# A one-token attention and MLP kernel on one core: wq loaded ahead of the first K group, masked blocks summed on VectorE, and eight more unused matrix products

## The chip, the core and the metric

The kernel runs on one core of one Trainium2 chip. The metric is the device time of one execution in microseconds; the time before is the median of three runs, 193.28 us (193.27 to 193.34). A profiled execution of the same kernel took 193.18 us; its trace spans 191.9 us from the first to the last instruction, so 1.28 us of the time lies outside the span.

## What is computed

Eight requests, one new token each, go through an attention block with a sliding window over cached K and V, and then through a token-mixing MLP. Cut to what matters (LN is a layer norm without weights):

```
q = LN(x) @ wq                                 # 8 x 512 by 512 x 4096: 32 heads of 128
k, v = k_cache[:, :, -2048:], v_cache[...]     # 8 requests x 8 kv heads x 2048 x 128, bf16
p = softmax(q . k / sqrt(128));  o = p . v     # 4 query heads share a kv head
h = x + o @ wo
# B block with one token: the shifted parts are zero, so hs = 0 and x1 = LN(h)
h2 = x1 + gelu(LN(x1) @ w3) @ w4               # 512 x 1792 and 1792 x 512
out = h + h2
```

The core reads 79.18 MB from HBM, nearly all of it K and V, and writes 8 KB.

## The kernel before

**Loads.** SyncE's queue (SP) issues every large load, one after another in program order, with a wait only where a buffer must first come free. K and V come in 16 groups each (four kv heads of one request, 2.10 MB); K has three buffers (`knat`), V has three (`vnat`). The order is the string at L777: the first K group, then wq (one large transfer into `wbig`, and six small ones into `wqF` that carry the last 1152 columns), then two more K groups, then V and K in turn, then wo in three pieces, w3, and w4 in three pieces (eight, four and two blocks of 128 rows). `load_k` (L745) waits until the TensorE transposes of the group three before are done, `load_v` (L750) until the P V products of the group three before are done, `load_wo` (L755) for the q products, `load_w3` (L767) for the transposes of q.

**K.** A group is four items. For each item TensorE transposes the K tile (`pe_T`, L374, eight products at L383), ScalarE evicts the lower half (L393) and VectorE the upper half (L395), and TensorE multiplies with q (`pe_QK`, L398). Every engine runs its instructions in the order of the source. The first four items' transposes (`AHEAD`, L606 to L608) stand in this order ahead of `q_rows` and `q_turn`, which compute q, scale it and transpose it (L278 to L344); `fill` (L346) puts q into its block form on GpSimd.

**Softmax and P V.** After eight items a request's scores go through `softmax_1` to `softmax_4` on VectorE and ScalarE, `turn_P` and `widen` bring P into place, and `pe_PV` (L497) makes 16 products with a V group. The result bank holds four blocks of 128 columns, of which a row needs one. VectorE multiplies with a mask (L514), two GpSimd additions sum the four blocks (L516, L517), and the sum `oacc` goes to `pe_O` (L526). For the last request VectorE does it in four instructions instead (L519, L522).

**The end.** After the last P V come the wo products (L553, L574), the mean and the squares over the features (L652, L683: products with ones), the 56 products with w3 (`pe_w3`, L673), the activation (L702 on VectorE, L704 on ScalarE), and the 56 products with w4 (L731) in three calls, one for each piece of w4, with eight products between the first and the second call that add the rest of the result (`pe_fin`, L717). Four copies (L741, L743) and one small store end the kernel.

**Unused products.** `warm` (L482) and `warm_end` (L490) put 128 x 128 by 512 bf16 products into TensorE's order that nobody reads (L485, L493). They write a PSUM bank that is free there, and wait for no late event. Ahead of w3 there are two of them behind the squares (L685).

Of the kernel before, what the change touches and what calls it, by code (L numbers as in the profile page):

```python
# [8 lines left out]
ALU = mybir.AluOpType  # L9
AX = mybir.AxisListType  # L10
# [69 lines left out]
def bass_sequential_preLN__sliding_block_cached__mixer_s_mlp__decode_kernel(  # L80
# [23 lines left out]
    with es:  # L104
# [173 lines left out]
        def q_rows():  # L278
            for k, rows, n, at, where in fills():
                a = xln_b[:, :]  # L280
                cols = bass.AP(tensor=a.tensor, offset=a.offset + KC * at + KC - 1, ap=[a.ap[0], [KC, k], [KC * k, 4]])
                e_xP = DV.op(lambda e, cols=cols, where=where: e.tensor_copy(
                    xlnP[:, where].rearrange("b (e a) -> b e a", a=4), cols))

            def pe_fT(e):
                for k, rows, n, at, where in fills():
                    ins = e.matmul(fT_ps[rows, n * B:(n + 1) * B], xlnP[:, where], ident_b[0:B, 0:B],
                                   is_transpose=True, tile_position=(0, rows.start))
                return ins
            e = PE.op(pe_fT, e_xP)  # L290
            for k, rows, n, at, where in fills():
                e_fT = DV.op(lambda e, rows=rows, n=n: e.tensor_copy(xlnF[rows, n, 0:B], fT_ps[rows, n * B:(n + 1) * B]),
                             e, e_fz)
            out = []
            for j in range(2):
                def pe_q(e, j=j):
                    for kc in range(KC):
                        for u in range(4):
                            n = (4 * j + u) * R * DH
                            size = R * DH if kc < KC - 1 else max(0, min(R * DH, H * DH - QF - n))  # L300
                            if size:
                                ins = e.matmul(S_ps[j][32 * u:32 * (u + 1), 0:size], xlnT[:, kc, :], wq_v[:, kc, n:n + size],  # L302
                                               start=(kc == 0), stop=(kc == KC - 1 and size == R * DH),
                                               tile_position=(0, 32 * u), skip_group_check=True)
                    return ins

                def pe_qF(e):
                    for n in range(NF):
                        for u in range(4):
                            w = (u - 4) * R * DH + QF  # L310
                            lo = max(0, -w)
                            if lo < R * DH:
                                ins = e.matmul(S_ps[1][32 * u:32 * (u + 1), lo:R * DH], xlnF[:, n, :],
                                               wqF[:, n, w + lo:w + R * DH], start=False, stop=(n == NF - 1),
                                               tile_position=(0, 32 * u), skip_group_check=True)
                    return ins
                e_q = PE.op(pe_q, e_xT, (sem_wq, 16))
                if j == 1:
                    e_q = PE.op(pe_qF, e_fT, (sem_wf, 16 * len(FILL)))
                got = S_ps[j][:, :].rearrange("p (r d) -> p r d", r=R)  # L320
                for c in range(2):
                    if j == 0:
                        e = AC.op(lambda e, c=c, got=got: e.activation(qrow2[:, 0, :, c, :], got, ACT.Copy, scale=inv_sqrt_dh),
                                  e_q)
                    else:
                        e = DV.op(lambda e, c=c, got=got: e.tensor_scalar(qrow2[:, 1, :, c, :], got, inv_sqrt_dh, None,
                                                                          ALU.mult), e_q)
                out.append(e)
            return out, e_q
# [160 lines left out]
        def warm_end(count):  # L490
            def f(e):
                for n in range(count):
                    ins = e.matmul(kbank[1], ident_b[:, :], still, start=True, stop=True)  # L493
                return ins
            PE.op(f, e_pT[LAST, 1])

        def pe_PV(m):  # L497
            b, q = divmod(m, NQ)
            at, bank = bank_of(q)

            def f(e):
                for n in range(NN):
                    u = n % 2
                    ins = e.matmul(bank[64 * u:64 * (u + 1), :],  # L504
                                   pT_sb[:, b % 2, n, :].rearrange("p (x q) -> p q x", q=NQ)[:, q, :],
                                   v_tile(m)[:, n * 512:(n + 1) * 512], start=(n < 2), stop=(n >= NN - 2),
                                   tile_position=(0, 64 * u), skip_group_check=True)
                return ins
            e_PV[m] = PE.op(f, V(m), *(e_pT[b, x] for x in range(KQ)), free[at])
            acc = oacc[:, b % 2, q, :]  # L510
            if b < LAST:
                a = own_s[:, :]
                own = bass.AP(tensor=a.tensor, offset=a.offset, ap=[a.ap[0], [1, NS], [0, DH]])
                free[at] = DV.op(lambda e: e.tensor_tensor(omask[:, :, :], bank.rearrange("p (s d) -> p s d", s=NS), own,  # L514
                                                           ALU.mult), e_PV[m], e_acc.get(m - 1), e_own_s)
                e = PO.op(lambda e: e.tensor_tensor(omask[:, 0:2, :], omask[:, 0:2, :], omask[:, 2:4, :], ALU.add), free[at], pool[-1])  # L516
                pool[-1] = e_acc[m] = PO.op(lambda e: e.tensor_tensor(acc, omask[:, 0, :], omask[:, 1, :], ALU.add), e, e_O.get(b - 2))  # L517
                return
            e = DV.op(lambda e: e.tensor_scalar(acc, bank[:, 0:DH], own_s[:, 0:1], None, ALU.mult),  # L519
                      e_PV[m], e_O.get(b - 2), e_own_s)  # L520
            for s in range(1, NS):
                e = DV.op(lambda e, s=s: e.scalar_tensor_tensor(acc, bank[:, s * DH:(s + 1) * DH], own_s[:, s:s + 1], acc,  # L522
                                                                ALU.mult, ALU.add), e)
            e_acc[m] = free[at] = e
# [74 lines left out]
        def quad(f, q):  # L599
# [3 lines left out]
                   (5, each(widen, 2)), (5, each(warm, 1)), (5, each(widen, 3)), (6, each(warm, 2)), (6, each(warm, 1))),  # L603
                  ((6, quad(pe_PV, 0)), (7, quad(pe_PV, 1)), (11, late_O), (8, last_O)))
        LAG = (0, 0, 0, 0, 0, 0, KQ, -1)
        for p in range(AHEAD):  # L606
            pe_T(p)
            evict(p)  # L608
        e_qrow, e_q = q_rows()
        e_qT, e_qturn = q_turn()  # L610
        fill(0)
        fill(1)
        for p in range(NITEM + 24):
# [59 lines left out]
        def pe_w3(lo, hi, *waits):  # L673
            def f(e):
                for fc in range(lo, hi):
                    n, f = divmod(fc, FH)
                    for kc in range(KC):
                        ins = e.matmul(y_ps[n][:, f * B:(f + 1) * B],  # L678
                                       w3_cols(kc, fc),
                                       uT[:, kc * B:(kc + 1) * B], start=(kc == 0), stop=(kc == KC - 1))  # L680
                return ins
            return PE.op(f, *waits)
        e_st2 = PE.op(lambda e: e.matmul(st2, ones_f[:, :], hsq[:, :], start=True, stop=True), e_sq,  # L683
                      free[2])
        warm_end(2)  # L685
        e_y = [pe_w3(0, FH, e_u, (sem_w3, 16)), pe_w3(FH, FC)]

        e_vs = DV.op(lambda e: e.tensor_reduce(vsum[:, :], vr(st2), AX.X, ALU.add), e_st2)

# [36 lines left out]
        for n, waits in enumerate(((*e_gT, free[1]), (), ())):  # L726
            lo, hi = W4_AT[n:n + 2]
            def pe_w4(e, lo=lo, hi=hi):
                for fc in range(lo, hi):
                    for nb in range(KC):  # L730
                        ins = e.matmul(z_ps[32 * nb:32 * (nb + 1), :], gT[:, fc, :],  # L731
                                       w4_sb[:, fc, nb * 128:(nb + 1) * 128], start=(fc == 0), stop=(fc == FC - 1),
                                       tile_position=(0, 32 * nb), skip_group_check=True)
                return ins
            if n == 1:
                pe_fin()
            e_z = PE.op(pe_w4, (sem_w4[n], 16), *waits)
        for nb in range(KC):
            to, got = out_sb[:, nb * 128:(nb + 1) * 128], z_ps[32 * nb:32 * nb + B, :]
# [34 lines left out]
                B_w4[lo * 128:hi * 128, :].rearrange("(g p k) n -> p g (k n)", p=128, k=k), sem_w4[n])  # L774

        turn = {"K": 0, "V": 0, "O": 0}
        for kind in "KQKK" + 9 * "VK" + "VKKVKVKVVVOVOO":  # L777
            if kind == "Q":
                load_wq()
                continue  # L780
            {"K": load_k, "V": load_v, "O": load_wo}[kind](turn[kind])
            turn[kind] += 1
# [42 lines left out]
```

## Time and profile before

| | |
|---|---|
| median of three runs | 193.28 us (193.27 to 193.34) |
| profiled execution, its time | 193.18 us |
| its span | 191.9 us |
| busy: TensorE, VectorE, ScalarE, GpSimd | 151.5, 102.5, 95.7, 30.3 us |
| chain that ended last: transfers | 65% of the span |
| mean granted TensorE clock | 0.939 |
| GpSimd's two additions per P V (L516, L517) | 726 and 455 ns, 14 times each |
| VectorE's mask (L514) | 686 to 692 ns, 14 times |
| last wait for w3, and end of the 56 products with it | 185.07, 187.06 us |
| last products with w4 begin, end | 189.36, 189.77 us |
| store issued | 190.50 us |

How to read it: busy time of an engine is the time its instructions took, whatever they stood behind. The chain that ended last is followed back from the last instruction, at each step to what released it. Times in tables of stretches are microseconds from the start of the span. The granted clock is the share of full speed that TensorE's clock had.

### The profile page before, as it was taken

What the parts mean: (1) busy time and instruction counts of PE and PEld (TensorE: products, weight loads), DVE (VectorE), ACT (ScalarE), POOL (GpSimd) and SP (SyncE); (2) the same over time, 40 slices, a digit from 0 to 9 for tenths busy, and PEclk for the clock granted to TensorE, in tenths of its full rate; (3) what the DMA queues carried; (4) which work ended last, traced back from release to release, by engine and by line L of the source; (5) the groups of instructions that cost most, each with busy time, mean ns of one, the idle gap of its engine ahead of it and who ended that gap; (6) DMA issues with size and microseconds to landing.
All of it is one profiled execution on the core that took longest, in us unless ns stands there. A gap on an engine that the chain in (4) does not pass through costs nothing.

```text
span 191.9 us, 3209 instructions
## 1 busy us (share of the span) xinstructions
PE 151.5 (79%) x1325; PEld 94.9 (49%) x1325; DVE 102.5 (53%) x245; ACT 95.7 (50%) x124; POOL 30.3 (16%) x65
## 2 busy tenths in 40 slices
PE   0293879988878998699978896989898994777874
PEld 0281247664546555465655463746554661323453
DVE  2754314773386438543775275646853885535323
ACT  3081127776272927284559263754782767420331
POOL 8300020100230023002300230024002200140030
PEclk9999769999996999889999997999999999999985
DMA  6999999999999999999999999999999999999991
GB/s 220 422 406 432 437 420 427 434 437 424 434 429 427 430 430 427 429 430 430 437 430 420 437 430 429 420 437 424 437 434 425 434 434 432 408 430 428 411 409 75
DMA packets 6478, 79.38 MB, mean 414 GB/s; under 512 B 688, under 2 KB 704, under 8 KB 1856
## 3 DMA queue, kind: packets, MB, share of 16 engines
q1 hardware_dynamic: 6448, 79.18, 97.2%
q8 instruction: 10, 0.16, 0.3%
q14 instruction: 4, 0.03, 0.0%
q10 hardware_dynamic: 16, 0.01, 0.0%
HBM read 79.18 MB, written 0.01 MB: 413 GB/s over the span
## 4 chain that ended last, share of the span: by engine, by line
DMA 65%; PE 22%; DVE 6%; ACT 4%; SPq 1%; issue 1%; POOL 0%
DMA knat<-in_A_k_cache_dram 31%; DMA w_sb<-in_B_w_dram 16%; DMA vnat<-in_A_v_cache_dram 10%; PE kT_ps L383 9%; DMA wbig<-in_A_wq_dram 8%; PE S_ps L504 3%; ACT pT_sb L472 2%; PE S_ps L408 2%; PE o_rows L504 2%; DVE kT_sb L395 2%; ACT kT_sb L393 1%; PE S_ps L302 1%; PE sm L529 1%; PE kT_ps L678 1%; SPq L207 1%
## 5 line engine op out<-in xcount | busy, mean ns | idle before, releaser
L393 ACT ACTIVATE kT_sb<-kT_ps 128x1024 bf16<-128x1024 bf16 x64 | 65.6, 1025 | 65.3 <-PE kT_ps L383 65.2
L383 PE MATMUL kT_ps<-turn_f,knat 128*128 128x128 f32 x512 | 76.5, 293 | 12.2 <-DMA knat<-in_A_k_cache_dram 9.6
L383 PEld LDWEIGHTS kT_ps<-turn_f,knat 128*128 128x128 f32 x512 | 60.4, 149 | 31.9 <-issue 13.4
L395 DVE COPY kT_sb<-kT_ps 128x1024 bf16<-128x1024 bf16 x64 | 43.9, 686 | 34.7 <-PE kT_ps L383 34.6
L516 POOL TENSOR_TENSOR omask<-omask 128x256 f32<-128x256 f32 x14 | 10.2, 726 | 113.3 <-DVE omask L514 113.3
L408 PE MATMUL S_ps<-kT_sb,qblk 128*32 128x512 bf16 x256 | 26.5, 408 | 1.7 <-POOL qblk L350 1.1
L504 PE MATMUL o_rows<-vnat,pT_sb 128*64 128x512 bf16 x128 | 15.4, 381 | 5.4 <-ACT pT_sb L472 5.4
L472 ACT ACTIVATE pT_sb<-o_rows,own_f 128x512 bf16<-128x512 f32 x28 | 17.7, 694 | 1.8 <-PE o_rows L467 1.6
L504 PE MATMUL S_ps<-vnat,pT_sb 128*64 128x512 bf16 x112 | 13.4, 382 | 0.7 <-DMA vnat<-in_A_v_cache_dram 0.7
L504 PEld LDWEIGHTS o_rows<-vnat,pT_sb 128*64 128x64 bf16 x128 | 8.0, 109 | 11.5 <-issue 7.7
L408 PEld LDWEIGHTS S_ps<-kT_sb,qblk 128*32 128x32 bf16 x256 | 6.6, 93 | 13.4 <-issue 8.3
L514 DVE TENSOR_TENSOR omask<-o_rows,own_s 128x512 f32<-128x512 f32 x7 | 4.8, 686 | 12.5 <-PE o_rows L504 12.5
L514 DVE TENSOR_TENSOR omask<-S_ps,own_s 128x512 f32<-128x512 f32 x7 | 4.8, 692 | 11.7 <-PE S_ps L504 11.7
L350 POOL COPY qblk<-qT 64x64 bf16<-64x64 bf16 x16 | 5.0, 312 | 27.0 <-DVE qT L342 16.4
L504 PEld LDWEIGHTS S_ps<-vnat,pT_sb 128*64 128x64 bf16 x112 | 5.8, 110 | 6.8 <-issue 1.6
L529 PE MATMUL sm<-oacc,sel_o 128*128 128x256 f32 x16 | 7.2, 537 | 0.6 <-DVE oX L536 0.6
L440 ACT ACTIVATE E_sb<-S_ps,negM 128x512 f32<-128x512 f32 x8 | 5.5, 689 | 2.4 <-DVE negM L436 2.4
L259 PE MATMUL sm<-ident_b,xln_b 8*128 8x8 bf16 x4 | 0.3, 176 | 8.0 <-DVE xln_b L234 8.0
L517 POOL TENSOR_TENSOR oacc<-omask 128x128 f32<-128x128 f32 x14 | 6.4, 455 | 1.1
L559 ACT ACTIVATE orow<-kT_ps 128x512 bf16<-128x512 f32 x1 | 0.6, 597 | 11.2 <-PE kT_ps L553 11.2
L431 DVE TENSOR_REDUCE mblk<-S_ps 128x1 f32<-128x512 f32 x8 | 5.5, 682 | 0.8 <-PE S_ps L408 0.8
L453 DVE STREAM_TRANSPOSE PT_sb<-P_sb 128x512 bf16<-128x512 bf16 x8 | 5.6, 702 | 0.0
(120 smaller groups left out, 102.6 us busy)
## 6 DMA issues: line engine op xcount, KB each, us to landing
knat<-in_A_k_cache_dram SPq DMA_DIRECT2D x16, 2048.0 KB, 19.3
vnat<-in_A_v_cache_dram SPq DMA_DIRECT2D x15, 2048.0 KB, 20.3
wbig<-in_A_wq_dram SPq DMA_DIRECT2D x1, 3808.0 KB, 16.1
wbig<-in_A_wo_dram SPq DMA_DIRECT2D x2, 1024.0 KB, 22.9
knat<-in_A_v_cache_dram SPq DMA_DIRECT2D x1, 2048.0 KB, 20.4
wbig<-in_A_wo_dram SPq DMA_DIRECT2D x1, 2048.0 KB, 24.7
w_sb<-in_B_w_dram SPq DMA_DIRECT2D x1, 1792.0 KB, 30.7
w_sb<-in_B_w_dram SPq DMA_DIRECT2D x1, 1024.0 KB, 32.6
```

What stands on the lines that cost most here:

```text
L383: ins = e.matmul(kT_ps[i % 2][:, n * 256:(n + 1) * 256].bitcast(dt.float32), knat[:, j % NK, c * DH:(c + 2) * DH].bitcast(dt.float32), tur ...
L393: e_lo[i] = AC.op(lambda e: e.activation(kT_sb[:, i % NKT, 0:W // 2], kT_ps[i % 2][:, 0:W // 2], ACT.Copy), e_Tlo[i], e_QK.get(i - NKT))
L395: e_hi[i] = DV.op(lambda e: e.tensor_copy(kT_sb[:, i % NKT, W // 2:W], kT_ps[i % 2][:, W // 2:W]), e_Thi[i], e_QK.get(i - NKT))
L408: ins = e.matmul(S_ps[b % 2][32 * t:32 * (t + 1), :], qblk[:, b % 2, KQ * q + t, half, at:at + H], kT[:, :, t, :, half], start=(q == 0 and ...
L431: e = DV.op(lambda e: e.tensor_reduce(mblk[:, 0:1], S_ps[b % 2][:, :], AX.X, ALU.max), e_QK[G * b + G - 1], e_mz)
L453: e_PT[b] = DV.op(lambda e: e.transpose(PT_sb[:, :], P_sb[:, :]), e_P[b], e_wide.get(b - 1))
L472: e_pT[b, t] = AC.op(lambda e: e.activation(pT_sb[:, b % 2, :, H * t:H * (t + 1)], bank[:, :].rearrange("p (n y) -> p n y", n=NN), ACT.Cop ...
L504: ins = e.matmul(bank[64 * u:64 * (u + 1), :], pT_sb[:, b % 2, n, :].rearrange("p (x q) -> p q x", q=NQ)[:, q, :], v_tile(m)[:, n * 512:(n ...
L514: free[at] = DV.op(lambda e: e.tensor_tensor(omask[:, :, :], bank.rearrange("p (s d) -> p s d", s=NS), own, ALU.mult), e_PV[m], e_acc.get( ...
L516: e = PO.op(lambda e: e.tensor_tensor(omask[:, 0:2, :], omask[:, 0:2, :], omask[:, 2:4, :], ALU.add), free[at], pool[-1])
L517: pool[-1] = e_acc[m] = PO.op(lambda e: e.tensor_tensor(acc, omask[:, 0, :], omask[:, 1, :], ALU.add), e, e_O.get(b - 2))
L529: e_O[b] = PE.op(lambda e: e.matmul(O_ps, sel_o[:, :], oacc[:, b % 2, :, :].rearrange("p q d -> p (q d)"), start=True, stop=True), e_acc[N ...
```

## The change

Four edits. At L516 and L517 the two GpSimd additions go, and one VectorE reduction over the four blocks takes their place. `q_rows` and `q_turn` move ahead of the first four items' transposes and evictions, on every engine, and the load string puts wq (Q) ahead of the first K. And three lines of unused products: five instead of two behind the squares, four new ones behind w3's products, one new one between `pe_fin` and the second call of w4's products.

```
-                e = PO.op(lambda e: e.tensor_tensor(omask[:, 0:2, :], omask[:, 0:2, :], omask[:, 2:4, :], ALU.add), free[at], pool[-1])
-                pool[-1] = e_acc[m] = PO.op(lambda e: e.tensor_tensor(acc, omask[:, 0, :], omask[:, 1, :], ALU.add), e, e_O.get(b - 2))
+                e_acc[m] = DV.op(lambda e: e.tensor_reduce(acc, omask[:, :, :].rearrange("p s d -> p d s"), AX.X, ALU.add),
+                                 free[at], e_O.get(b - 2))
...
+        e_qrow, e_q = q_rows()
+        e_qT, e_qturn = q_turn()
         for p in range(AHEAD):
             pe_T(p)
             evict(p)
-        e_qrow, e_q = q_rows()
-        e_qT, e_qturn = q_turn()
...
-        warm_end(2)
+        warm_end(5)
         e_y = [pe_w3(0, FH, e_u, (sem_w3, 16)), pe_w3(FH, FC)]
+        warm_end(4)
...
             if n == 1:
                 pe_fin()
+                warm_end(1)
             e_z = PE.op(pe_w4, (sem_w4[n], 16), *waits)
...
-        for kind in "KQKK" + 9 * "VK" + "VKKVKVKVVVOVOO":
+        for kind in "QKKK" + 9 * "VK" + "VKKVKVKVVVOVOO":
```

## The prediction

> **What bounds the kernel now.** I read the page's slices first, then the table of DMA queues.
>
> ```profile
> PEclk9999769999996999889999997999999999999985
> DMA  6999999999999999999999999999999999999991
> GB/s 220 422 406 432 437 420 427 434 437 424 434 429 427 430 430 427 429 430 430 437 430 420 437 430 429 420 437 424 437 434 425 434 434 432 408 430 428 411 409 75
> ...
> q1 hardware_dynamic: 6448, 79.18, 97.2%
> ```
>
> The 16 DMA engines are busy from the first slice to the last but one, at about 430 GB/s, and SP's one queue carries nearly all of it. 79.18 MB at 430 GB/s are 184 us of the 191.9. So the kernel is a stream, with a start of about 2 us and an end. The engines matter in two places only: where they let the queue run dry, and behind the last bytes. Then the chain that ended last, in order of time, for the end:
>
> ```profile
> 154.37 30.67 DMA w_sb<-in_B_w_dram
> 185.03 0.05 issue
> 185.08 1.99 PE kT_ps L678 x56
> ...
> 187.74 1.05 PE S_ps L731 x24
> ```
>
> From 154.37 everything is issued, and the chain is one transfer until w3 lands at 185.03. The timeline shows what holds after that:
>
> ```profile
> 187.74 1.05 PE L731 MATMUL S_ps<-w_sb,qrow 128*32 128x128 bf16 x32 [0.68 <-ACT qrow L704]
> 188.54 0.45 PE L721 MATMUL S_ps<-ident_b,qrow 128*32 128x128 bf16 x8
> ...
> 188.76 1.01 PE L731 MATMUL S_ps<-w_sb,qrow 128*32 128x128 bf16 x24
> 189.36 0.14 PEld L731 LDWEIGHTS S_ps<-w_sb,qrow 128*32 128x32 bf16 x8 [0.21 <-DMA w_sb<-in_B_w_dram]
> ```
>
> The last line decides: before w4's last eight products TensorE waits 0.21 us for the last bytes of the kernel. What TensorE does earlier is worth nothing so long as it is ready by 189.3; behind that come 0.41 us of products, then copies and store.
>
> **Part 1, wq ahead of K.** SP's order changes, its bytes and instructions do not. The first K group (2.10 MB) takes 2.10 / 0.43 = 4.9 us, so wq lands at 17.5 - 4.9 = 12.6 instead of 17.5, and the K group behind wq and its six small transfers at about 19. On TensorE the q work stood behind the first transposes and still waited for wq:
>
> ```profile
> 17.57 2.75 PE S_ps L302 x29
> ...
> 20.35 1.48 PE S_ps L313 x6
> ...
> 21.86 1.30 DVE w_sb L326 x2
> ...
> 23.20 0.67 PE sm L336 x4
> ```
>
> That is 6.3 us from 17.57 to 23.87; from 12.6 it ends at 18.9. Then the first four items' transposes, which took 5.6 us (8.59 to 14.19, paced by the evictions), run from 19.2 to 24.8; the fill of q on GpSimd (0.65 us) lies beside them; two items' products (0.9 us) follow, and the fifth item begins at about 25.7, against 25.82 now. So TensorE meets the rest of the stream where it did. The cost is in SP's queue: the fourth K load waits for these transposes and goes from 14.21 to 24.8, with its followers behind it. Issued before it: wq 4.19 MB and four groups, 12.58 MB, which last until 2.3 + 12.58 / 0.43 = 31.6. It is 6.8 us early instead of 17. If these transposes ran at half clock all the time (11.2 us) it would be 30.4, still in time. ScalarE and VectorE have the q evictions ahead of the K evictions, but the K group lands later than these end. Part 1 costs 0; if the cover went (K4 later than 31.6), each us would cost one us of stream. Below nothing: the queue could start 0.07 us sooner, as wq's issue took 0.57 and K's 0.64 us. I take 0.
>
> **Part 2, the sum on VectorE.** Off GpSimd: 14 x (726 + 455) ns = 16.5 us. On VectorE: 14 reductions of 128x512 f32 to 128x128. No row shows this form; nearest is the reduction 128x1 from 128x512 (L431, 682 ns). Lower end 486 ns (L450, 512 columns to bf16), upper end four times a 128-column reduction over groups of four (L241, 352 ns), 1.4 us. I take 0.7: 9.8 us more on an engine that is busy 102.5 of 191.9. The result comes sooner (two additions and their hand-over took 1.34 us, 145.19 to 146.53). Behind the reduction in VectorE's order stands mostly an eviction (L395), which TensorE's next transposes wait for: each P V can push TensorE by up to 0.7 (1.4) us. The cover is the queue. Its narrowest place now is the V load issued at 88.85: before it 4.19 MB and 17 groups were issued, 39.84 MB, which last until 2.3 + 39.84 / 0.43 = 95. That leaves 6.2 us, and TensorE waits for K 9.6 us in all, so a delay does not add up from request to request. At the end: the last such reduction starts at 169.5 and ends by 170.9 at most; the next VectorE work (L519) starts at 171.59. Cost 0.
>
> **Part 3, eight products more.** One such product takes 0.217 us behind another: four took 1.03 us at 175.55, the last 0.379. The three behind the squares run from 184.03 to 184.7, in TensorE's idle time before w3 lands (0.89 us of it): 0. At half clock all five would take 2.2 us and hold w3 up until 185.8. The four behind w3 begin at 186.9, where w3's last product was issued, and end at 187.78 at full clock; w4 began at 187.74. One more behind `pe_fin`: 0.22. What they are for is read from the stretches between two possible steps of the clock. Its steps lie on a grid of 3.41 us (117.36, 120.77, ... 185.62), for instance:
>
> ```profile
> 158.32:161.73 3.41, 2.03 (x19) 0.77 (x17) 1.96 (x3) 2.02 (x3) 0.00 (x0) 1.00 0.95 408
> ...
> 182.21:185.62 3.41, 2.31 (x25) 1.23 (x25) 1.06 (x7) 1.60 (x3) 1.46 (x2) 1.00 1.03 419
> 185.62:189.03 3.41, 2.73 (x97) 2.64 (x98) 1.10 (x6) 0.50 (x3) 0.46 (x1) 0.50 0.67 267
> ```
>
> Behind the second the clock fell, though its busy time is the larger one: small products count little. Its 512-column products are four, 0.87 us or 25%; with three more it holds seven, 45%. The first stretch, behind which the clock stayed, holds (three transposes, three rounds of L408, one L467) about 1.2 us or 36%. So I expect full clock until the end. What is that worth? Not w3: its 56 products came every 33 ns on both sides of 185.62. w4's came in fours every 107 ns at half clock; at full clock between 53 and 107, no row shows it. w4's first call then ends at 187.8 + 0.43 to 0.86, `pe_fin` 0.11 to 0.21, the unused product 0.22, the second call (not before its bytes, 188.75) 0.21 to 0.43: ready between 188.98 and 189.5, for bytes at 189.32. Behind these: eight products, 0.05 us sooner by their spacing at best, and the last one 0.047 shorter (267 against 314 ns). Worth -0.10 to +0.2; I take -0.07, the bytes deciding.
>
> **Sum.** 0 + 0 - 0.07: 193.11 on the profiled execution's 193.18, 193.2 on the median of 193.28, with 193.05 to 193.5 for this case. A measurement of this kernel tells about 0.2%, 0.39 us, from no change, so this is "same".
>
> **Rivals.** *The clock falls in the end (slower).* In the new order four unused products stand between w3 and w4. If the clock falls before 186.9, these take 4 x 0.43 = 1.73 us and w4 begins at 188.65; then 0.86 + 0.21 + 0.43 + 0.43 + 0.21 at the spacing shown, and 0.25 for the last: 191.05 instead of 189.77, so 193.28 + 1.28 = 194.56. If it falls at 187.8, about 0.4, 193.7. It decides where the stretch of 3.41 us that ends in 186.4 to 187.8 is too empty: it would hold five to five and a half products and small ones, 35 to 40%, just at the 36% that was enough. For it: the nearness, and that the grid may lie elsewhere in another run. Against it: in this trace's grid the steps are 185.62 and 189.03. The Trainium skill, TensorE: Matmul & The Clock Gate, Part 1, has a window of 3413 ns that runs freely and does not start with the kernel; the trace agrees with the length (the 64.85 us between the steps at 120.77 and 185.62 are 19 of them); one trace cannot show the rest. By that rule runs of the same kernel would differ, some at the forecast and some near this rival's time. The chance: the grid was seen in one run only; if it lies anywhere, 1.4 of 3.41 us of its positions put a step there, about half of them bad, and some more put one near 183.4, ahead of the five products: 0.26. This is also the case in which the products don't do what they say.
>
> *The stream ends sooner (faster).* The DMA engines don't end together:
>
> ```profile
> 186.50:187.00 0.50, 0.50 (x19) 0.47 (x16) 0.00 (x0) 0.21 (x1) 0.00 (x0) 0.50 0.89 361
> 187.00:187.50 0.50, 0.06 (x3) 0.00 (x0) 0.37 (x3) 0.16 (x1) 0.00 (x0) 0.50 0.82 328
> 187.50:188.00 0.50, 0.27 (x12) 0.29 (x16) 0.43 (x3) 0.09 (x1) 0.00 (x0) 0.50 0.61 229
> 188.00:188.50 0.50, 0.50 (x32) 0.50 (x24) 0.07 (x1) 0.00 (x0) 0.00 (x0) 0.50 0.36 139
> ```
>
> With 0.95 before and 0.18 after, 1.1 us of all 16 are idle from 186 to 189. A new order that evened them out could bring half of that, 192.7. Against it: every engine has the same bytes in either order. 0.10.
>
> *The queue runs dry (slower).* K4 after 31.6, by 1 us: 194.3. Against it: 6.8 us of room. 0.04.
>
> **Numbers.** Forecast 0.60, clock 0.26, dry 0.04, sooner 0.10. Faster by over 0.2%: 0.10 and a little of the forecast's edge, 0.12; slower: 0.28; within: 0.60. The range leaves out most of the faster case and the worst of the clock's: 192.9 to 194.4.
>
> **What would show it.** The last load of w4's weights behind a wait for DMA at 189.3 still: stream unchanged. Full granted clock to 189: part 3. K4's issue near 25, and no slice of DMA below 9 before 186: part 1. A reduction near 0.7 us and no later V loads than 5 us: part 2. Wrong if w4's first product begins after 188 (clock), or if the last bytes move by more than 0.3 us.

## The result, and the profile after

The changed kernel takes 192.90 us (median of 13 runs, 192.78 to 193.06), the kernel before, measured beside it, 193.32 us (13 runs, 193.18 to 193.52). The ratio is 0.9979 with an interval of 0.9972 to 0.9986: 0.4 us faster. The interval does not reach 1, but the gain is only the 0.2% that the prediction names as the bound of what can be told from no change. The forecast was 193.2, 0.08 us faster. The profiled execution took 193.02 us, with a span of 191.6 us against 191.9. As the profiled execution of the kernel before (193.18) was as fast as its fastest run, the two profiles are 0.16 us apart, and show less than the 0.42 us between the medians.

The page of the kernel after, the lines that answer to those shown first: granted clock, DMA share and GB/s in 40 slices, and SP's queue.

```profile
PEclk9999999957999999789999999999999999699999
DMA  6999999999999999999999999999999999999991
GB/s 224 452 400 431 434 414 434 438 429 431 428 424 434 424 434 434 433 421 431 431 434 421 434 434 434 424 431 428 429 428 431 438 424 431 428 431 415 413 406 74
...
q1 hardware_dynamic: 6448, 79.18, 97.3%
```

It is the same stream: the same packets and bytes, and no slice of DMA below 9 from the second to the last but one. The second slice has 452 GB/s instead of 422; the other slices differ both ways. The clock no longer falls in the last two slices.

The end, from the timeline of the kernel after (start, duration, engine, line, what it does, and in brackets the wait before it):

```profile
184.94 1.96 PE L678 MATMUL kT_ps<-uT,w_sb 128*128 128x8 bf16 x56 [0.16 <-DMA w_sb<-in_B_w_dram]
...
186.76 1.02 PE L493 MATMUL kT_ps<-ident_f,ident_b 128*128 128x512 bf16 x4
...
187.71 0.63 PE L732 MATMUL S_ps<-w_sb,qrow 128*32 128x128 bf16 x32
...
188.71 0.81 PE L732 MATMUL S_ps<-w_sb,qrow 128*32 128x128 bf16 x24
189.22 0.12 PEld L732 LDWEIGHTS S_ps<-w_sb,qrow 128*32 128x32 bf16 x8 [0.28 <-DMA w_sb<-in_B_w_dram]
```

The last eight weight loads still wait for the last bytes of w4, as before: until 189.22 instead of 189.36. The stream ends sooner, and no engine's work explains that. The clock edit has worked (w4's first call takes 0.63 us, not 1.05), yet TensorE is ready for bytes that are not there. So the question was where the stream gained its time.

The first difference stands at the start. SP's issues in the timelines, first the kernel before, then the kernel after:

```profile
0.72 0.64 SPq L207 DMA_DIRECT2D knat<-in_A_k_cache_dram  x1
1.42 0.57 SPq L207 DMA_DIRECT2D wbig<-in_A_wq_dram  x1
```

```profile
0.72 0.40 SPq L207 DMA_DIRECT2D wbig<-in_A_wq_dram  x1
1.18 4.74 SPq L207 DMA_DIRECT2D w_sb<-in_A_wq_dram  x6
5.96 1.92 SPq L207 DMA_DIRECT2D knat<-in_A_k_cache_dram  x3
7.92 0.61 SPq L207 DMA_DIRECT2D vnat<-in_A_v_cache_dram  x1
24.78 0.54 SPq L207 DMA_DIRECT2D knat<-in_A_k_cache_dram  x1
```

wq's issue takes 0.40 us in the first place; it had taken 0.57 in the second. K's took 0.64. And the stretches just behind, before and after (from:to and length, then busy time of PE, PEld, DVE, ACT and POOL, granted clock, DMA share, GB/s):

```profile
1.60:1.80 0.20, 0.00 (x0) 0.00 (x0) 0.00 (x0) 0.20 (x1) 0.20 (x1) 1.00 0.13 41
1.80:2.00 0.20, 0.00 (x0) 0.00 (x0) 0.00 (x0) 0.20 (x1) 0.20 (x1) 1.00 0.00 0
```

```profile
1.60:1.80 0.20, 0.00 (x0) 0.00 (x0) 0.00 (x0) 0.20 (x1) 0.20 (x1) 1.00 2.62 650
1.80:2.00 0.20, 0.00 (x0) 0.00 (x0) 0.00 (x0) 0.20 (x1) 0.20 (x1) 1.00 3.21 762
```

A packet is booked whole where it starts (the share of 3.21 shows it), so 762 GB/s is a burst of starts and no rate. What counts is the moment: the queue's first packets start at 1.73 instead of 2.13 us. The Trainium skill, DMA: Bandwidth & Descriptors, "Latency and other measured facts", gives about 600 ns to the first byte of a transfer from such a queue; counted from the end of the issue it was 0.61 us for wq, which agrees, and 0.77 for K.

Spread over the time that each packet took, the bytes landed show a lead over the kernel before of 0.07 MB at 2.5 us, none at 5 us (wq's first packets, of 30 KB, took up to 2.2 us against 1.13 us later; K's, of 16 KB, up to 1.1 against 0.61), 0.035 MB at 10 us, 0.115 MB at 20 us, and then 0.09 to 0.13 MB until 186 us. At 0.43 MB per us, 0.115 MB is 0.27 us. The last bytes of w4 land 0.15 us sooner (189.17 against 189.32), and TensorE's last eight products, at full clock, take 0.32 instead of 0.41 us.

### The profile page after: what moved, and what is told of

The parts are those of the page before. It is cut to its first block, busy times and chain, and to the rows that moved or that the text cites. A ratio compares the mean times of both kernels' runs of the same rounds, so it can differ in the third digit from the quotient of the medians.

```text
span 191.6 us, 3183 instructions
## 1 busy us (share of the span) xinstructions
PE 153.1 (80%) x1326; PEld 94.7 (49%) x1333; DVE 116.5 (61%) x259; ACT 95.6 (50%) x124; POOL 13.7 (7%) x37
## 4 chain that ended last, share of the span: by engine, by line
DMA 55%; PE 20%; SPq 8%; DVE 8%; ACT 6%; issue 1%
DMA knat<-in_A_k_cache_dram 29%; DMA vnat<-in_A_v_cache_dram 11%; DMA w_sb<-in_B_w_dram 10%; SPq L207 8%; PE kT_ps L383 8%; DMA wbig<-in_A_wq_dram 6%; ACT kT_sb L393 3%; ACT pT_sb L472 3%; PE o_rows L504 3%; PE S_ps L504 3%; DVE kT_sb L395 2%; PE S_ps L302 2%; DVE oacc L516 2%; PE S_ps L408 2%; DVE omask L514 1%
## 5 line engine op out<-in xcount | busy, mean ns | idle before, releaser
L383 PEld LDWEIGHTS kT_ps<-turn_f,knat 128*128 128x128 f32 x512 | 59.5, 147 | 35.0 <-issue 13.0
L504 PE MATMUL o_rows<-vnat,pT_sb 128*64 128x512 bf16 x128 | 16.5, 402 | 4.9 <-ACT pT_sb L472 4.9
L516 DVE TENSOR_REDUCE oacc<-omask 128x128 f32<-128x512 f32 x14 | 14.9, 1064 | 0.5
L323 ACT ACTIVATE w_sb<-S_ps 128x512 bf16<-128x512 f32 x2 | 1.1, 594 | 11.4 <-PE S_ps L302 11.4
L529 PE MATMUL sm<-oacc,sel_o 128*128 128x256 f32 x16 | 6.1, 466 | 0.6 <-DVE oX L536 0.6
L431 DVE TENSOR_REDUCE mblk<-S_ps 128x1 f32<-128x512 f32 x8 | 5.5, 682 | 0.8 <-PE S_ps L408 0.8
```

The source lines that it names most:

```text
L383: ins = e.matmul(kT_ps[i % 2][:, n * 256:(n + 1) * 256].bitcast(dt.float32), knat[:, j % NK, c * DH:(c + 2) * DH].bitcast(dt.float32), tur ...
L431: e = DV.op(lambda e: e.tensor_reduce(mblk[:, 0:1], S_ps[b % 2][:, :], AX.X, ALU.max), e_QK[G * b + G - 1], e_mz)
L504: ins = e.matmul(bank[64 * u:64 * (u + 1), :], pT_sb[:, b % 2, n, :].rearrange("p (x q) -> p q x", q=NQ)[:, q, :], v_tile(m)[:, n * 512:(n ...
L516: e_acc[m] = DV.op(lambda e: e.tensor_reduce(acc, omask[:, :, :].rearrange("p s d -> p d s"), AX.X, ALU.add), free[at], e_O.get(b - 2))
L529: e_O[b] = PE.op(lambda e: e.matmul(O_ps, sel_o[:, :], oacc[:, b % 2, :, :].rearrange("p q d -> p (q d)"), start=True, stop=True), e_acc[N ...
```

## The experiments

The first theory after the result was that order and end work together: the order lands the last bytes sooner, the full clock shortens what stands behind them. After the first four runs it became: the gain is the stream's earlier start, made by the order of the loads alone; sum and products are hidden. Rivals: the sum gives it (GpSimd's work gone, engines free sooner), or the products do (full clock in the end). Times are medians. The kernel before was measured beside each group of runs: 193.31 us beside the first four of the table, 193.28 beside the next four, 193.38 beside the last four.

| kernel | us (range, runs) | ratio to before (interval) |
|---|---|---|
| order alone | 192.96 (192.85 to 193.27, 11) | 0.998 (0.9972 to 0.9989) |
| sum alone | 193.28 (193.16 to 193.44, 11) | 1.0 (0.9991 to 1.0008) |
| products alone | 193.28 (193.04 to 194.99, 12) | 1.0013 (0.9992 to 1.0035) |
| change without the five | 194.35 (193.84 to 194.72, 4) | 1.005 (1.0034 to 1.0067) |
| load string alone | 194.1 (193.56 to 195.21, 12) | 1.0041 (1.0024 to 1.0057) |
| engines' order alone | 193.42 (193.19 to 193.89, 11) | 1.0008 (1.0 to 1.0017) |
| a piece of wq, K, the rest | 193.33 (193.01 to 194.97, 12) | 1.0019 (0.9996 to 1.0042) |
| the change again | 192.95 (192.76 to 193.84, 12) | 0.9987 (0.9976 to 0.9998) |
| the change with the five only | 193.03 (192.88 to 193.24, 11) | 0.9986 (0.9977 to 0.9994) |
| order and sum, no products | 193.01 (192.88 to 193.4, 11) | 0.9984 (0.9975 to 0.9992) |
| the change, each reduction twice | 194.18 (193.12 to 195.85, 12) | 1.0055 (1.0023 to 1.0087) |
| the change, a tiny transfer first | 193.43 (193.11 to 195.0, 12) | 1.0024 (1.0002 to 1.0046) |

**Order alone.** Kernel before, with `q_rows` and `q_turn` ahead of the first transposes, and the string:

```
-        for kind in "KQKK" + 9 * "VK" + "VKKVKVKVVVOVOO":
+        for kind in "QKKK" + 9 * "VK" + "VKKVKVKVVVOVOO":
```

> The kernel before with the new order alone (wq ahead of the first K group, q's work ahead of the first transposes). Theory, order and end together: the last bytes land about 0.15 us sooner, as they did in the profile after (w4's last weights behind a wait that ends at 189.22 instead of 189.36), and the time falls by 0.1 to 0.2 us; the last eight products still run at half clock where the clock falls at 185.6. Rival, products alone: no change within 0.05 us, last wait at 189.36. Rival, the sum alone (one instruction fetch fewer beside the stream): no change either.

192.96: all of the gain but 0.06, and more than the 0.1 to 0.2 us expected. Its clock does fall in the end (w4's first call takes 1.04 us), and its last wait ends at 189.05 all the same. Here the lead is 0.18 MB from 20 us on.

**Sum alone.** Kernel before, with the reduction at L516.

> The kernel before with the sum on VectorE alone. Theory, order and end together: 0 within 0.05 us; the reduction takes 1.06 us as in the profile after, no load is issued too late, last wait at 189.36. Rival, the sum alone: the last bytes 0.1 to 0.2 us sooner and the time down by as much, with three instead of four fetches in the second instruction queue.

193.28, no change. The rival that the sum gives the gain falls.

**Products alone.** Kernel before, with the eight products.

> The kernel before with the eight unused products alone. Theory, order and end together: granted clock full to the end, the last bytes where they were, 0.09 us less behind them (0.32 instead of 0.41 us for the last eight products), so 0.1 us faster, and up to 0.2 if the copies begin sooner as well. Rival, products alone: all of the 0.4 us. Rival, the clock falls in some runs: runs of 193.7 and more among the others.

193.28, where 0.1 us faster was expected. Nine runs lie between 193.04 and 193.35, three at 194.68, 194.82 and 194.99. So the products alone give nothing that shows, and one run in four pays about 1.5 us. The mean granted clock of these three is 0.912 to 0.930, that of the nine 0.938 to 0.963: they lose clock somewhere. None of them was profiled, so that the clock fell in the end there is argued.

**The change without the five products behind the squares** (the four and the one stay, and the two of before go as well):

```
-        warm_end(5)
         e_y = [pe_w3(0, FH, e_u, (sem_w3, 16)), pe_w3(FH, FC)]
         warm_end(4)
```

> The changed kernel without the products behind the squares, and with those behind w3 and ahead of w4's second call: what the four cost where the clock falls. Theory: the clock falls before or in the four, these take up to 1.73 us instead of 0.86, and the time is up to 1.28 us above the kernel before, less by what the order gives: 193.7 to 194.5, different from run to run with the place of the step. Rival, the four have cover at half clock too: 193.0 to 193.2.

194.35. In the profiled run of this kernel the stretches between two steps of the clock, and its timeline, are:

```profile
179.98:183.39 3.41, 3.17 (x67) 2.23 (x63) 1.47 (x6) 1.88 (x2) 0.00 (x0) 1.00 1.03 423
183.39:186.80 3.41, 2.17 (x59) 1.98 (x59) 0.61 (x3) 1.83 (x3) 1.92 (x2) 0.50 0.99 405
186.80:190.21 3.41, 3.41 (x49) 1.46 (x51) 0.88 (x5) 0.25 (x1) 0.00 (x0) 0.50 0.25 97
```

```profile
186.62 1.87 PE L493 MATMUL kT_ps<-ident_f,ident_b 128*128 128x512 bf16 x4
...
188.42 1.04 PE L731 MATMUL S_ps<-w_sb,qrow 128*32 128x128 bf16 x32
...
190.15 0.53 PE L731 MATMUL S_ps<-w_sb,qrow 128*32 128x128 bf16 x24
```

The clock fell at 183.39, though TensorE was busy for 3.17 of the 3.41 us before: busy time alone does not tell when it falls, which fits the prediction's reading that small products count little. The stretch behind it, 2.17 us busy, did not bring it back; in the run with a tiny transfer first, below, a stretch at half clock that held most of the five was busy throughout (3.42 us), and the clock came back behind it. So the four take 1.87 us instead of 1.02, w4 begins at 188.42 instead of 187.71, and its last two calls run from 190.15, long after the bytes (landed at 189.06). This is the rival "the clock falls in the end" at work: span 192.8 instead of 191.6 us.

**The load string alone**, `"QKKK"` with the engines' order as before.

> The load order alone (wq ahead of the first K group), the engines' order as before. Theory, the first issue: SP's first instruction takes 0.40 instead of 0.64 us and data flow from 1.7 instead of 2.1 us, which nobody waits for on an engine; the time falls by 0.3 to 0.4 us as with both moves, since the queue still never runs dry (fifth K load near 38 us, dry at 41). Rival, the engines' order: TensorE's better start is what counts; then this gives 0.

Missed: 194.1 us, 0.8 slower. The lead is there (0.14 MB at 20 us), but q now waits in TensorE's order behind transposes whose K lands 11 us later (19.27 instead of 8.23), and SP waits with it. SP's issues in this kernel's timeline:

```profile
25.39 0.54 SPq L207 DMA_DIRECT2D knat<-in_A_k_cache_dram  x1
25.97 0.60 SPq L207 DMA_DIRECT2D vnat<-in_A_v_cache_dram  x1
38.38 0.53 SPq L207 DMA_DIRECT2D knat<-in_A_k_cache_dram  x1
...
53.66 0.54 SPq L207 DMA_DIRECT2D vnat<-in_A_v_cache_dram  x1
```

Two dips stand in its stretches (the kernel before has 420 to 438 GB/s in the same five):

```profile
40.00:44.00 4.00, 3.69 (x36) 2.67 (x32) 3.10 (x8) 3.00 (x5) 0.62 (x2) 1.00 0.98 410
44.00:48.00 4.00, 3.21 (x25) 2.13 (x26) 3.54 (x9) 3.10 (x5) 0.00 (x0) 1.00 0.97 414
48.00:52.00 4.00, 3.39 (x32) 2.26 (x34) 1.71 (x3) 3.76 (x6) 0.00 (x0) 1.00 1.03 438
52.00:56.00 4.00, 4.00 (x38) 2.34 (x36) 1.38 (x2) 1.51 (x2) 1.19 (x2) 1.00 0.96 410
56.00:60.00 4.00, 4.00 (x37) 2.67 (x34) 2.66 (x7) 2.05 (x2) 1.81 (x4) 1.00 0.96 403
```

From 36 to 60 us the lead of 0.15 MB becomes an arrear of 0.15, 0.7 us of stream; the DMA share of 0.96 to 0.98 is read as some engines that had run out of work. The arrear, 0.35 us, is what the profiled run is slower (193.63 against 193.28); the other runs, up to 195.21, were not profiled. By the prediction's sum the load at 38.38 was in time: wq and six groups, 16.77 MB, last until 2.3 + 16.77 / 0.43 = 41.3. So that sum, with the mean rate, overstates the room. With 3 us left by it (and 2.2 at the load at 53.66, ahead of the second dip) the queue runs dry in part; with 6.8 us, as in the change, it does not.

**The engines' order alone**, the string as before.

> The engines' order alone (q's work ahead of the first transposes), the loads as before. Theory, the first issue: 0 within 0.1 us; the fourth K load goes out at about 17.5 + 6.3 + 5.6 = 29.5 us, 2 us before the queue runs dry at 31.6. Rival, the engines' order: 0.35 us faster. Rival, the cover is thinner than its sum says: slower, by what the queue stands idle near 31 us.

193.42: no gain, and 0.08 MB of arrear from 36 us on; the fourth K load went out at 28.39, by the sum 3.2 us ahead of the dry queue. The two halves of the edit need each other: the string puts the stream ahead, the engines' order keeps the queue filled.

**A piece of wq first** (0.52 MB, with its own semaphore), then K, then the rest of wq:

```
+            dma(SP, wbig[:, 0:QP], A_wq.rearrange("(p k) n -> p (k n)", k=KC)[:, 0:QP], sem_wq0)
...
+        for kind in "PKQKK" + 9 * "VK" + "VKKVKVKVVVOVOO":
```

> The kernel before with a piece of wq (0.52 MB, 4 KB of each partition) as the very first load, then K's first group, then the rest of wq. Theory, the first issue: the quick issue of a simple row transfer starts the stream 0.4 us sooner, whatever comes second: 0.2 to 0.3 us faster, though wq lands as late as before. Rival, the place of the six small transfers or of the large rows in the stream: no change, as these stand where they stood.

Divided, and as a whole no gain: six runs at 193.01 to 193.13, 0.2 us faster as the theory says, two at 193.5 and four at 194.6 to 195.0. The profiled run was one of the long ones. In it one of the 16 DMA engines lagged: from the first K group on, the last of a transfer's 16 parts came some 1.5 us behind the others (wq's at 19.27 against 17.44 us), and so did the last bytes of w4 (190.83). Why is open. The first packets of this run do start at 1.75 us, as in the change; none of the six short runs was profiled.

**The change again.**

> The changed kernel once more, to count runs in which the clock falls in the end: with the products alone 3 of 12 runs took 194.7 to 195.0 us, in 13 runs of the changed kernel none did. Theory, the grid of the clock lies anywhere: one run in five to ten near 194.4 here too, the others at 192.9. Rival, the new order or the sum moved the end out of reach: none.

192.95: eight runs at 192.76 to 193.0, the others at 193.21, 193.28, 193.59 and 193.84. In all 25 runs of the change none lies near 194.6. The two longest are near the 193.7 that the prediction has for a clock that falls at 187.8; neither was profiled. In the profiled run (192.90 us) the end no longer waits for the stream. TensorE's products with the last V and those of w4's last two calls, from its timeline:

```profile
173.66 1.90 PE L504 MATMUL S_ps<-knat,pT_sb 128*64 128x512 bf16 x16
...
188.88 0.59 PE L732 MATMUL S_ps<-w_sb,qrow 128*32 128x128 bf16 x24
```

No wait for a transfer stands there (the 24 take 0.59 instead of 0.81 us), and the last transfer in the chain that ended last lands at 146.31 us, though the last bytes of w4 land at 189.13, much as in the first profile. So in the change TensorE's own work and the stream end almost together, and either can be last.

**The change with the five only.**

```
         e_y = [pe_w3(0, FH, e_u, (sem_w3, 16)), pe_w3(FH, FC)]
-        warm_end(4)
...
-                warm_end(1)
```

> The change with only the five products behind the squares; the four behind w3 and the one behind the rest sum are gone. Theory (the gain comes from the order of the loads alone, and the end waits for the last bytes): 192.95, as the change. Where the clock stays, w4 begins 0.9 us earlier and still waits for its bytes at about 189.1; where it falls at some point after 186, nothing unused stands in the way, so no run at 194.4 or above. Rival (the four and the one keep the clock up and are worth something): 193.1 to 193.3, with the end as in the order alone, w4's last calls at half clock.

**Order and sum, none of the eight products.**

> Order and sum of the change, with the two unused products behind the squares as before and none of the eight. Theory: 192.95 to 193.05, the whole of the change's gain, as the order alone gave 192.96 and the sum alone nothing; the clock falls in the end and the last wait is still that for the last bytes near 189.1. Rival (the reduction on VectorE needs the queue's cover and costs something beside the new order, and the products give it back): 193.2 or more.

193.03 with the five only, 193.01 without the eight; both as expected, and in both profiles the last weight loads wait for the last bytes. One reading was missed: with the five only, w4 does not begin 0.9 us earlier (187.64 against 187.71), as it waits there for the activation; the four unused products fill this wait. With 192.90 and 192.95 for the change, the products are worth about 0.1 us at most, which is less than one comparison can tell. None of these 22 runs lies above 193.4.

**Each reduction twice.**

```
                 e_acc[m] = DV.op(lambda e: e.tensor_reduce(acc, ..., AX.X, ALU.add),
                                  free[at], e_O.get(b - 2))
+                e_acc[m] = DV.op(lambda e: e.tensor_reduce(acc, ..., AX.X, ALU.add),
+                                 e_acc[m])
```

> The change with each of the 14 reductions on VectorE made twice, the second over the first with the same result: 14 x 1.06 = 14.9 us more on VectorE, which was busy 116.5 of 191.6. Theory (the queue covers it, with some 6 us at its narrowest place by the mean rate): the V loads move by up to 1 to 3 us, the time stays within 0.2 us of the change, 192.95 to 193.15. Rival (the room is much smaller than that sum says, as the run with the load order alone ran dry with 3 us of room left by the same sum): the queue runs dry and the time goes up by 0.5 us or more, 193.5 to 195.

Divided, and the theory missed: six runs at 193.12 to 193.54, six at 194.81 to 195.85. In the profiled run, one of the short six (193.26 us), the queue never ran short: its V loads come 1.5 us sooner to 1.5 us later than in the change, and its lead over the kernel before is about 0.15 MB from 20 us to 186 us. What has gone is another cover, TensorE's wait for the last V group. First the kernel before, then the change (its first profile), then this kernel, all from the timeline of PE:

```profile
173.17 1.92 PE L504 MATMUL S_ps<-knat,pT_sb 128*64 128x512 bf16 x16 [1.63 <-DMA knat<-in_A_v_cache_dram]
```

```profile
173.11 1.92 PE L504 MATMUL S_ps<-knat,pT_sb 128*64 128x512 bf16 x16 [0.48 <-DMA knat<-in_A_v_cache_dram]
```

```profile
173.79 1.90 PE L504 MATMUL S_ps<-knat,pT_sb 128*64 128x512 bf16 x16
...
185.48 0.69 PE L680 MATMUL kT_ps<-uT,w_sb 128*128 128x8 bf16 x17
```

Without a wait in brackets TensorE no longer meets the stream there: it comes late by its own work, at 173.79, and w3's products begin at 185.48 without a wait for w3. What TensorE then loses, the end loses: a further stretch at half clock would no longer be hidden. The six long runs have a mean granted clock of 0.947 to 0.956, the six short ones 0.964 to 0.982. That this is where their 1.5 to 2.5 us lie is argued; none of them was profiled.

**A tiny transfer first**, 64 KB of wq, the rest behind it:

```
+        QP = 256
...
+        for kind in "PQKKK" + 9 * "VK" + "VKKVKVKVVVOVOO":
```

> The change with a first transfer of 64 KB cut from wq (the first 256 columns of each partition's row) and the rest behind it: one transfer more is issued ahead of the stream, which starts with 0.15 us worth of bytes. Theory (a late start of the stream is paid one for one): the tiny transfer's issue takes about 0.40 us, the rest's issue ends at about 1.75 instead of 1.12 us, and 0.15 us of it is covered by the tiny one's bytes: 0.4 to 0.5 us later, 193.35 to 193.45. Rival (the first bytes come at the same moment whatever is issued first, and the gain lies in the place of the transfers behind): 192.95 to 193.05.

193.43, where the theory had 193.35 to 193.45, but the runs spread: seven from 193.11 to 193.5, five from 194.07 to 195.0. That the median falls there is in part luck. The two issues took 0.87 us together, and the same stretches as above show the later start:

```profile
1.60:1.80 0.20, 0.00 (x0) 0.00 (x0) 0.00 (x0) 0.20 (x1) 0.20 (x1) 1.00 0.24 74
1.80:2.00 0.20, 0.00 (x0) 0.00 (x0) 0.00 (x0) 0.20 (x1) 0.20 (x1) 1.00 0.55 164
```

At 20 us it has 0.16 MB less than the change, 0.38 us, and keeps this until 186 us. So a later start of the stream is not made up in bytes. What it costs in time, this run does not show by itself: in it (193.5 us) the clock also fell close to the end:

```profile
182.03:185.45 3.42, 3.42 (x17) 1.60 (x14) 1.16 (x7) 1.19 (x3) 0.77 (x2) 0.50 1.03 421
185.45:188.80 3.35, 3.35 (x79) 2.46 (x81) 1.09 (x6) 1.20 (x3) 1.15 (x1) 1.00 0.74 295
```

The five products ran at half clock, w3 began at 185.83 without a wait for its bytes, and w4's last products had no wait for theirs: the price that the prediction gave for this ("hold w3 up until 185.8").

No version beat the change.

## Why the prediction was nearly right, and where it failed

The measured 192.90 us lies on the lower edge of the range (192.9 to 194.4), and the gain is 0.42 us where 0.08 was forecast. That the time was met so nearly is in part luck: the terms of the sum did not give this gain.

**What bounds the kernel**: right for the kernel before, and with the order or the products alone: the last weights wait for the last bytes. In the change it holds in the first profile; in the second, TensorE's own work ends as late as the stream and nothing waits.

**Part 1**: the step that failed is "Below nothing: the queue could start 0.07 us sooner, as wq's issue took 0.57 and K's 0.64 us. I take 0." The term was named and put at nothing: the order alone gives 0.35 us (193.31 to 192.96). The 0.57 us was the duration of wq's issue in the second place, behind K's; in the first it takes 0.40, and the first packet starts 0.40 us sooner. That explains the lead in the first 2.5 us. It does not explain all that is kept. By 5 us the lead is gone in some kernels (the change) and not in others (0.05 MB in the order alone), and most of it opens between 5 and 20 us. By 20 us all eight profiled kernels that load wq whole and first had a lead of 0.11 to 0.18 MB, and the three others with the old string were at -0.03 to +0.01. One difference stands in all of these traces: with the old string the stream falls to 351 to 401 GB/s between 17 and 18 us, where wq and its six small transfers end, and with the new one to 410 to 421 between 12 and 13 us (bytes spread over each packet's time). In the kernel before that is some 0.03 MB; where the rest comes from is open. So it is shown that the order of the loads, with the engines' order to match, makes the gain; that the earlier start is all of it is not. The rest of the part held: the fourth K load was issued at 24.78 us (24.8 was predicted), and no slice of DMA fell below 9. But the room of 6.8 us is overstated, as the load string alone ran short with 3 us of it left.

**Part 2**: cost 0, right (the sum alone: 193.28 against 193.31), but with a longer reduction and another cover than named. The group of the reduction in the kernel after:

```profile
L516 DVE TENSOR_REDUCE oacc<-omask 128x128 f32<-128x512 f32 x14 | 14.9, 1064 | 0.5
```

1064 ns, where 0.7 was taken from bounds of 0.486 and 1.4 us. The prediction looked at the queue's room (6.2 us), which the change hardly used: the V load of 88.85 us is issued at 88.56. It overlooked that the wait for the last V, 1.63 us, and the one for w3, 0.89 us, were the cover for all that TensorE loses late. The order alone leaves 1.02 us of the first, the sum alone 0.52, the change 0.48 us, and in the second profiled run of the change, as in that without the products, nothing is left of it. The reductions twice, with six of twelve runs at 194.81 us or more, make it likely that the edit is one step from costing something.

**Part 3**: not contradicted: about 0.1 us at most beside the new order and nothing alone, for -0.07 taken; no comparison tells so little from 0. Full clock until the end was right in both profiled runs of the change. Its last eight products took 0.32 us instead of 0.41.

**The rival of the clock** is real in other kernels, and its price was near: 1.28 us predicted, about 1.5 in three of twelve runs of the products alone (not profiled), 1.4 in the change without the five against the change (194.35 to 192.95). That it took none of 25 runs of the change in full, and perhaps two in its smaller form, was not foreseen (0.26 would have been six), and why stays open. The ground for it held: the steps lie elsewhere in each run. Carried on by 3.41 us to the same stretch they were at 185.62 (before), 185.00 (after), 184.12, 184.34, 183.39 and 185.42 us in others, as the Trainium skill, TensorE: Matmul & The Clock Gate, "What's actually happening", says of its free-running window; here runs show it.

**The stream ends sooner** came true in its effect, 0.4 us, but the mechanism named, evened ends of the DMA engines, is not what the traces show: the stream is ahead from 20 us on. The last bytes moved by 0.15 us in the change and by 0.31 in the order alone, where the prediction gave more than 0.3 as a sign of being wrong.

## What to carry to other kernels

In a kernel that is one stream from the first transfer to the last, the first issue lies on the path: bytes that start late stayed late here, to the end. Try the transfer that is quickest to issue in the first place, but let the engines' order follow it: without that the queue ran short later, and the kernel was 0.8 us slower. When work is moved onto an engine, look for its cover in every wait up to the end, not only in the narrowest place of the queue, and double the work once to see how much of the cover is left.

## What the runs showed of the hardware

- The issue of one transfer is not of one length: wq 0.40 us in the first place and 0.57 in the second, K 0.64 in the first, 0.62 in the second (the piece of wq first) and 0.54 after a wait.
- The first packets of this kernel are slow: wq's of some 30 KB took up to 2.2 us, against 1.13 us later, and K's of 16 KB up to 1.1 us, against 0.61.
- A reduction over a strided last axis (128x512 f32 to 128x128) took 1064 ns, one over a contiguous axis of as many elements (L431, which reads S_ps and writes one result per partition) 682 ns.
- A queue with bytes for 2 to 3 us left by the mean rate ran at 403 to 414 GB/s instead of 430.
- One DMA engine can lag for a whole run by some 1.5 us. It was seen in one profiled run, which took 194.69 us, and its cause is open.
